# Routed attention and squared-ReLU layer, one core: the first head pair's loads, turns and one-hot rows rearranged

## The chip, the core and the metric

The kernel runs on one core of one Trainium2 chip. The metric is the device time of one execution in microseconds (us). Engines are named as the profile names them: PE is TensorE's matmul stream and PEld its weight loads, DVE is VectorE, ACT is ScalarE, POOL is GpSimd, and SP is SyncE, which here only issues DMAs. "SPq" and "ACTq" mark instructions that an engine's sequencer handles itself, above all DMA issues.

## What is computed

```python
q_n, k_n, c_n = each / (norm(each, axis=-1) + 1e-6)
q_assign = argmax(einsum('bhsd,hcd->bhsc', q_n, c_n), -1)   # nearest of 16 centroids
k_assign = argmax(einsum('bhsd,hcd->bhsc', k_n, c_n), -1)
scores = where(q_assign == k_assign, q @ k.T / sqrt(D), -1e9)
x = (softmax(scores) @ v)           # (4, 8, 768, 64) -> (3072, 512)
out = relu(x @ w_in) ** 2 @ w_out   # 512 -> 2048 -> 512
```

Batch 4, 8 heads, sequence 768, head width 64, all fp32.

## The kernel before

**Pairs.** The 32 (batch, head) problems are worked as 16 pairs of heads; the two heads of a pair share the 128 partitions. For each pair PE needs the queries and keys turned (head width on the partitions): the tile `qkT`, [128, 12, 128], 6 blocks of queries, then 6 of keys. From it come

- `logits(pair)` (L319): centroid scores of queries and keys; DVE turns them (`turn_logits`, L330) and finds the nearest centroid (`number`, L335);
- the mask, as a small matmul of rows that encode the centroid numbers (`mask`, L431). For pair 0 these rows are one-hot rows, turned on PE (`turn_onehot`, L378); for the others three rows per head that go through DRAM: `far` (L370) and then two DMAs into a `rows` tile (L373);
- `score` (L421), whose products PE adds in the same PSUM tile `sc`; then ACT's exponential (L442) and PE's product with v (`times_v`, L455), in the banks V and M.

There are three `sc` tiles of two PSUM banks each, and the two single banks V and M (`av_a`, `av_b` in the profile): eight banks together.

**Three ways to turn.** Pair 0 is turned on PE by `turn_first` (L259), pair 1 on PE by `turn` (L276), and from pair 2 on the DMA does it: `split_words` (L294) has ACT take the fp32 words apart into a tile `flat` and SP write it to DRAM (L303), once for the queries and once for the keys; `turn_words` (L310) reads both back with a transposing DMA (L314).

**The prologue.** SP and ACT issue the loads (L154 to L159): the centroids and the first keys on ACT's queue, everything else on SP's. POOL makes the identity `ident`, PE multiplies it by itself eight times (L170, the fp32 matmul is two records each, so 16 rows), and DVE fills constants, among them `oh` (L211) and two `rows` tiles (L218). Then, in the order in which they are written: `centroids_norm` (DVE, with a square root and a loaded exponential table on ACT), `turn_first(0)` for the queries, `turn_first(1)` for the keys, `centroids_turned` (one PE transpose into M, copied by DVE to `cnT`), `logits(0)`, `turn_logits(0)`, `number(0)`.

**What sets the order.** From L164 on, every engine's instructions stand in the order in which the program states them; semaphores are put in automatically. The loop of pairs is L575 to L660. For pair 0 the order is, after the loads of pair 3, three weight blocks and v of pair 1 on SP:

```python
for i in range(2):
    turn(1, i, (V, M)[i])
    score(p, i, 0, True)
split_words(2, 0)
turn_onehot()
turn(1, 2, V)
# masks and exponentials 0 to 2, logits(1), number(1), tiles 3 to 5
split_words(2, 1)
turn_words(2)
split_words(p + 3, 0)
# tiles 6 to 8
split_words(p + 3, 1)
load_qk(p + 4, (nc.scalar, nc.scalar))
round_1(p)
# times_v, evict, add_up; then pair 1: its tiles 0 to 2, logits(2), ...
```

`load_qk(4)` is issued by ACT; `round_1` (L128) is the first step of rounding a block of `w_in` on ACT; `evict` (L465) copies a finished product out of V or M. The tiles that take q, k and `flat` share six buffers (`loads`, tag `qk`).

After the 16 pairs come the two matrix products (L742 and L794), which are most of the time.

Of the kernel before, what the change touches and what calls it, by code (L numbers as in the profile page):

```python
# [8 lines left out]
F32 = mybir.dt.float32  # L9
BF16 = mybir.dt.bfloat16  # L10
# [3 lines left out]
ALU = mybir.AluOpType  # L14
# [4 lines left out]
P = 128  # L19
# [6 lines left out]
def kernel(  # L26
# [55 lines left out]
    def load_qk(pair, queues=(nc.sync, nc.sync)):  # L82
        if pair >= NG:
            return
        b, hp = divmod(pair, HP)
        raw[pair] = []
        for name, src, queue in zip(("q_raw", "k_raw"), (q, k), queues):
            t = loads.tile([P, 2, NCH, D], F32, name=name, tag="qk")
            queue.dma_start(
                t, src[b, 2 * hp : 2 * hp + 2].rearrange("h (p j) d -> p h j d", p=P)  # L90
            )
            raw[pair].append(t)
# [55 lines left out]
    def round_3(i):  # L148
        dst, lo, hi = of_block(i)
        raw_w.pop(i)  # L150
        dst, lo = dst.bitcast(I32), lo.bitcast(I32)
        nc.gpsimd.tensor_tensor(out=dst, in0=dst, in1=lo, op=ALU.add)  # L152

    cen = once.tile([P, D], F32, name="cen")  # L154
    nc.scalar.dma_start(cen, centroids.rearrange("h c d -> (h c) d"))
    load_qk(0, (nc.sync, nc.scalar))
    for pair in range(1, BY_PE + 1):
        load_qk(pair)
    load_v(0)  # L159

# [3 lines left out]
        tc.manual_schedule(engines={E.PE, E.DVE, E.Activation, E.Pool, E.SP})  # L164
    )

    ident = const.tile([P, P], F32, name="ident")
    make_identity(nc, ident)
    warm_up = ps_sc.tile([P, 2, 512], F32, name="sc")
    for _ in range(8):  # L170
        nc.tensor.matmul(warm_up[:, 0, 0:P], lhsT=ident, rhs=ident, start=True, stop=True)  # L171
    ident_b = const.tile([P, P], BF16, name="ident_b")
    nc.vector.tensor_copy(out=ident_b, in_=ident)
    ups = const.tile([P, D], F32, name="ups")
# [39 lines left out]
    marks = once.tile([P, 3, 32], BF16, name="marks")  # L214
    nc.vector.memset(marks, 0.0)
    rows_of = [once.tile([P, 2, S], BF16, name=f"rows_{i}") for i in range(2)]
    for t in rows_of:
        nc.vector.memset(t, 0.0)  # L218

    cnT = const.tile([P, H * C], F32, name="cnT")  # L220
    cn = const.tile([P, 2, D], F32, name="cen_n")
# [26 lines left out]
            )  # L248

    def centroids_turned():  # L250
        nc.tensor.transpose(
            out=M[:, 0:P], in_=cn.rearrange("p e d -> p (e d)"), identity=ident
        )
        nc.vector.tensor_copy(out=cnT, in_=M[:, 0:P])

    qkT = {}
    ohT = {}

    def turn_first(which):  # L259
        if which == 0:  # L260
            qkT[0] = qktp.tile([P, 2 * NCH, P], F32, name="qkT")
        pt = ps_sc.tile([P, 2, 512], F32, name="sc")
        for c in range(NCH):
            for e in range(2):
                nc.tensor.matmul(  # L265
                    pt[D * e : D * (e + 1), c // NB, (c % NB) * P : (c % NB + 1) * P],
                    lhsT=raw[0][which][:, e, c], rhs=ident, start=True, stop=True,
                )
        for i in range(2):
            copy = nc.vector.tensor_copy if which and i else nc.scalar.copy  # L270
            c = NCH * which + NB * i
            copy(out=qkT[0][:, c : c + NB].rearrange("p c n -> p (c n)"), in_=pt[:, i, 0:TB])
        if which == 1:
            raw.pop(0)

    def turn(pair, part, bank):  # L276
# [17 lines left out]
    def split_words(pair, which):  # L294
        if pair >= NG:
            return
        if which == 0:
            words[pair] = dram.tile([2 * NCH, P, 2, 2 * D], U16, name="words")
        flat = loads.tile([P, NCH, 2, 2 * D], U16, name="flat", tag="qk")
        src = raw[pair][which].bitcast(U16).rearrange("p h c (d two) -> p h c two d", two=2)  # L300
        for e in range(2):
            nc.scalar.copy(out=flat[:, :, :, D * e : D * (e + 1)], in_=src[:, e])
        nc.sync.dma_start(  # L303
            words[pair][NCH * which : NCH * (which + 1)].rearrange("c p two d -> p c two d"),
            flat,
        )
        if which == 1:
            raw.pop(pair)
# [10 lines left out]
    def logits(pair, bank):  # L319
        hp = pair % HP  # L320
        for g in range(4):
            nc.tensor.matmul(  # L322
                bank[32 * g : 32 * g + 32, 0, 0:TB], lhsT=cnT[:, 2 * C * hp : 2 * C * (hp + 1)],
                rhs=qkT[pair][:, NB * g : NB * (g + 1)], start=True, stop=True,
            )
# [52 lines left out]
    def turn_onehot():  # L378
        spare = expp.tile([P, 2, 512], F32, name="ex").bitcast(BF16)
        ohT[0] = spare.rearrange("p a n -> p (a n)")[:, 0 : 2 * S].rearrange(  # L380
            "p (a n) -> p a n", a=2
        )
        po = sc.pop("oh").rearrange("p a n -> p (a n)").bitcast(BF16)[:, 0 : NBL * P]
        po = po.rearrange("p (b g i) -> p b g i", b=NBL, g=4)
        for b in range(NBL):
            nc.tensor.transpose(
                out=po[:, b].rearrange("p g i -> p (g i)"),
                in_=oh[:, b].rearrange("p e c -> p (e c)"), identity=ident_b,
            )
        for which in range(2):  # L390
            dst = ohT[0][:, which].rearrange("p (g b i) -> p b g i", g=2, b=NBL)
            src = po[:, :, 2 * which : 2 * which + 2]
            if which == 0:
                nc.scalar.copy(out=dst, in_=src)
            else:
                nc.vector.tensor_scalar(
                    out=dst, in0=src, scalar1=BIG, scalar2=-BIG, op0=ALU.mult, op1=ALU.add
                )

# [14 lines left out]
    def begin(i):  # L416
        sc[i] = ps_sc.tile([P, 2, 512], F32, name="sc")
        return sc[i]
# [142 lines left out]
            loaded += 1  # L561

    centroids_norm()
    turn_first(0)
    turn_first(1)
    centroids_turned()
    logits(0, begin("ls"))
    for i in ("oh", 0, 1):
        begin(i)
# [5 lines left out]
    for p in range(NG):  # L575
        if p == 0:
            load_qk(3)
            load_ahead(0)
        if p == HP + 1:
            nc.sync.dma_start(x_far, xT.pop(0))  # L580
        if p:
            invert(p - 1)
            turn_words(p + 2)
            spread(p - 1)
        if 2 < p + 1 < NG:
            turn_logits(p + 1)
            number(p + 1)
        load_v(p + 1)
        if p:
            load_ahead(p - 1)  # L590


        if p == 0:
            for i in range(2):
                turn(1, i, (V, M)[i])
                score(p, i, 0, True)
            split_words(2, 0)
            turn_onehot()
            turn(1, 2, V)
            for i in range(NB):  # L600
                if i == 2:
                    begin(i)
                    score(p, i, 0, True)
                mask(p, i, 0, False)
                exponential(i)
        else:
            for i in range(NB):
                tile_of(p, i)
        total[p] = endp.tile([P, 2, S], F32, name="total")
        first, last = total[p][:, :, 0:QA], total[p][:, :, QA:S]  # L610
        add(nc.vector, first, ex[0], ex[1])
        if p < 2:
            logits(p + 1, begin("ls"))
            turn_logits(p + 1)
            number(p + 1)
        add(nc.vector, first, first, ex[2])
        for i in range(NB, NCH):
            tile_of(p, i)
            add(nc.vector, first, first, ex[i])
        if p == 0:  # L620
            split_words(2, 1)
            turn_words(2)
        split_words(p + 3, 0)


        for i in range(NCH, NCH + NB):
            tile_of(p, i)
        part = accp.tile([P, 2, 512], F32, name="part")
        add(nc.vector, part, ex[NCH], ex[NCH + 1])
        add(nc.vector, part, part, ex[NCH + 2])  # L630
        add(nc.vector, last, part[:, :, 0:QB], part[:, :, QB : 2 * QB])
        if p:
            finish(p - 1)
            round_2(p - 1)
            round_3(p - 1)
        split_words(p + 3, 1)
        load_qk(p + 4, (nc.scalar, nc.scalar))
        round_1(p)


        for i in range(NCH):
            times_v(p, i, V)
        evict(p, 0, V)
        for i in range(NCH, NCH + NB):
            times_v(p, i, M)
        raw_v.pop(p)
        if p + 1 < NG:
            bank = begin("ls")
            if 2 < p + 2:
                if p + 2 < NG:  # L650
                    logits(p + 2, bank)
            add_up(p, bank[:, 1])
        evict(p, NCH, M)
        for d in (qkT, ohT):
            d.pop(p)
        if p >= NG - 2:
            for _ in range(2):
                if (found := next(x_early)) is not None:
                    first_sums.append(found)
            w_early.append(w_sums(len(w_early)))  # L660
# [407 lines left out]
```

## Time and profile before

| | us |
|---|---|
| median of 3 runs (lowest to highest) | 913.22 (913.16 to 913.4) |
| the profiled execution: device time | 913.43 |
| its span, first to last instruction | 911.6 |
| PE busy | 899.4 |
| DVE, ACT, POOL busy | 581.7, 316.2, 150.1 |
| first matmul of `logits(0)` | 10.09 |
| first mask matmul of pair 0 | 17.49 |
| first matmul of `logits(2)` | 38.50 |

The difference between device time and span, 1.83 us, lies before the first and behind the last instruction. All times in the text are us from the first instruction. In rows of the timeline and the chain the first number is the start, the second the busy time. A row merges equal instructions; where the text goes into single instructions, it uses the trace's own rows. "Landed" is when a DMA's last semaphore increment stands in the trace.

### The profile page before, as it was taken

The numbers are of one execution on the slowest core, as the hardware profiler recorded it, in microseconds if no ns is written. First come the engines' busy times: TensorE is split into PE (matmuls) and PEld (weight loads), VectorE is DVE, ScalarE is ACT, GpSimd is POOL, SyncE is SP. The second block draws the span as 40 slices with busy tenths as digits, with TensorE's granted clock in tenths as the row PEclk, the third lists the DMA queues.
The fourth block names the chain that finished last, engine by engine and source line by source line (L and its number), as shares of the span: only waits on it lengthen the run. The fifth ranks groups of instructions, "written<-read, shape, count | busy, mean of one in ns | idle before, by whom it ended". The sixth has DMA issues, their size and how long they took to land.

```text
span 911.6 us, 11728 instructions
## 1 busy us (share of the span) xinstructions
PE 899.4 (99%) x4543; PEld 578.8 (63%) x4543; DVE 581.7 (64%) x930; ACT 316.2 (35%) x457; POOL 150.1 (16%) x168
## 2 busy tenths in 40 slices
PE   8999999999999999899999999999999999999997
PEld 5444444444444455478875568886558887557886
DVE  5798888888888999994326565225655333656321
ACT  5876677776776567530001110001110000111000
POOL 0000100001000267710023310023220003240000
PEclk9999999999999999999999999999999999999999
DMA  7677778777673154110000000000000000000000
GB/s 261 154 191 220 218 214 208 179 210 213 172 177 86 61 184 139 41 70 24 24 24 0 1 0 19 18 19 16 1 1 0 24 24 24 0 1 0 24 24 27
DMA packets 98482, 75.03 MB, mean 82 GB/s; under 512 B 54666, under 2 KB 89074, under 8 KB 98162
## 3 DMA queue, kind: packets, MB, share of 16 engines
q1 hardware_dynamic: 91474, 64.33, 24.9%
q10 hardware_dynamic: 6944, 9.86, 3.4%
q8 instruction: 38, 0.62, 0.3%
q14 instruction: 26, 0.21, 0.1%
HBM read 43.83 MB, written 19.34 MB: 69 GB/s over the span
## 4 chain that ended last, share of the span: by engine, by line
PE 92%; DVE 5%; issue 1%; ACT 1%; POOL 0%; DVEq 0%; POOLq 0%
PE bank L794 32%; PE bank L742 28%; PE sc L426 12%; PE av_a L459 9%; PE av_b L459 4%; PE sc L435 3%; PE sc L322 1%; DVE w_raw L137 1%; PE sc L478 1%; DVE g L699 1%; DVE w_raw L140 1%; DVE total L445 1%; DVE xT L510 0%; PE sc L171 0%; PE sc L265 0%
## 5 line engine op out<-in xcount | busy, mean ns | idle before, releaser
L699 DVE TENSOR_TENSOR g<-bank,g 128x384 f32<-128x384 f32 x192 | 102.9, 553 | 90.8 <-PE bank L742 88.6
L442 ACT ACTIVATE ex<-sc 128x1024 f32<-128x1024 f32 x144 | 144.2, 1025 | 39.0 <-PE sc L426 34.1
L426 PE MATMUL sc<-qkT 64*128 64x512 f32 (+1 forms) x768 | 150.6, 484 | 0.0
L794 PE MATMUL bank<-w_out,g 128*128 128x256 f32 x576 | 127.2, 379 | 0.0
L794 PEld LDWEIGHTS bank<-w_out,g 128*128 128x128 f32 x576 | 109.4, 190 | 15.7
L699 DVE TENSOR_TENSOR osb<-bank,osb 128x256 f32<-128x256 f32 x72 | 29.3, 422 | 136.5 <-PE bank L794 125.9
L742 PE MATMUL bank<-x_t,w_s 128*128 128x384 f32 x256 | 93.3, 487 | 3.1 <-POOL w_s L522 3.1
L742 PE MATMUL bank<-xT,w_in 128*128 128x384 f32 x256 | 93.2, 487 | 0.0
L742 PE MATMUL bank<-xT,w_s 128*128 128x384 f32 x256 | 93.0, 486 | 0.0
L426 PEld LDWEIGHTS sc<-qkT 64*128 64x128 f32 x768 | 65.9, 188 | 41.9 <-issue 30.1
L794 PE MATMUL bank<-w_t,g_s 128*128 128x256 f32 x384 | 86.8, 379 | 0.0
L794 PE MATMUL bank<-w_t,g 128*128 128x256 f32 x384 | 86.8, 379 | 0.0
L459 PE MATMUL av_a<-ex,v_raw 128*64 128x512 f32 x384 | 85.9, 596 | 0.0
L542 POOL TENSOR_TENSOR w_s<-w_in 128x256 f32<-128x256 f32 x32 | 26.7, 835 | 351.3 <-PE bank L794 235.4
L445 DVE TENSOR_TENSOR total<-total,ex 128x1024 f32<-128x1024 f32 x64 | 78.7, 1229 | 6.5
L705 ACT COPY osb<-bank 128x256 f32<-128x256 f32 x12 | 4.5, 372 | 216.1 <-PE bank L794 216.1
L794 PEld LDWEIGHTS bank<-w_t,g_s 128*128 128x128 f32 x384 | 73.0, 190 | 9.9
L794 PEld LDWEIGHTS bank<-w_t,g 128*128 128x128 f32 x384 | 73.0, 190 | 9.9
L705 ACT COPY g<-bank 128x384 f32<-128x384 f32 x32 | 15.3, 477 | 173.9 <-PE bank L742 173.9
L742 PEld LDWEIGHTS bank<-x_t,w_s 128*128 128x128 f32 x256 | 48.4, 190 | 37.9 <-POOL w_s L522 4.8
L152 POOL TENSOR_TENSOR w_in<-w_in,w_raw 128x512 int32<-128x512 int32 x16 | 22.1, 1378 | 296.4 <-DVE w_in L144 296.4
L742 PEld LDWEIGHTS bank<-xT,w_s 128*128 128x128 f32 x256 | 48.6, 190 | 33.9
(128 smaller groups left out, 1021.5 us busy)
## 6 DMA issues: line engine op xcount, KB each, us to landing
words<-flat SPq DMA_DIRECT2D x28, 384.0 KB
w_raw<-in_moe_w_in_dram SPq DMA_DIRECT2D x16, 512.0 KB
w_raw<-in_moe_w_out_dram SPq DMA_DIRECT2D x16, 512.0 KB
v_raw<-in_v_dram SPq DMA_DIRECT2D x16, 384.0 KB
rb<-far_r SPq DMA_DIRECT2D x32, 192.0 KB
out_dram<-osb SPq DMA_DIRECT2D x23, 256.0 KB
k_raw<-in_k_dram ACTq DMA_DIRECT2D x13, 384.0 KB
q_raw<-in_q_dram ACTq DMA_DIRECT2D x12, 384.0 KB
```

Of the source, the lines that this page charges most:

```text
L137: nc.vector.scalar_tensor_tensor(out=lo, in0=hi, scalar=0x80000000, in1=lo, op0=ALU.bitwise_and, op1=ALU.bitwise_or)
L152: nc.gpsimd.tensor_tensor(out=dst, in0=dst, in1=lo, op=ALU.add)
L426: nc.tensor.matmul(sc[i][:, e, cols], lhsT=qkT[pair][rows, NCH + c], rhs=qkT[pair][rows, n.start // P : n.stop // P], start=first, stop=no ...
L435: nc.tensor.matmul(sc[i][:, e, cols], lhsT=ohT[pair][rows, 1, c * P : (c + 1) * P], rhs=ohT[pair][rows, 0, columns(i)], start=first, stop= ...
L442: nc.scalar.activation(out=ex[i], in_=sc.pop(i), func=ACT.Exp, scale=SCALE)
L445: eng.tensor_tensor(out=out, in0=a, in1=b, op=ALU.add)
L459: nc.tensor.matmul(bank[D * e : D * (e + 1), 0 : n.stop - n.start], lhsT=raw_v[pair][:, e, c], rhs=ex[i][:, e, cols], start=c == 0, stop=c ...
L542: nc.gpsimd.tensor_tensor(out=s1, in0=a[1][0], in1=a[1][1], op=ALU.add)
L699: nc.vector.tensor_tensor(out=out, in0=bank, in1=to, op=ALU.add)
L705: nc.scalar.copy(out=c11, in_=bank)
L742: nc.tensor.matmul(bank, lhsT=operands[j][0][:, kk], rhs=operands[j][1][:, kk], start=(kk == 0), stop=(kk == H2 - 1),)
L794: nc.tensor.matmul(bank, lhsT=left[:, f], rhs=right[:, f], start=(f == 0), stop=(f == F2 - 1))
```

## The change

1. The first keys are loaded on SP's queue behind the first queries, and no longer on ACT's queue.
2. PE's eight first matmuls multiply a tile of zeros, filled by DVE's first instruction, and no longer wait for `ident`.
3. The two `rows` tiles (DVE, L218) are filled after `turn_onehot`, and no longer ahead of the centroids' norm.
4. `turn_first` works in halves of three blocks, each in a bank of its own: the queries in V and M, the keys in one bank each of two `sc` tiles. ACT copies the first three halves and DVE the last. The transpose of the centroids stands between the two halves of the keys, in the second bank of the tile of the first matmuls.
5. `turn_onehot` works in two halves of six blocks: the first in the `sc` tile's bank, copied by ACT (query rows and key rows), the second in M, copied by DVE (both).
6. `split_words(2, 0)` moves from ahead of `turn_onehot` to behind tiles 3 to 5, next to `split_words(2, 1)`; the two halves of pair 3 move behind tiles 6 to 8.

```diff
-    load_qk(0, (nc.sync, nc.scalar))
-    for pair in range(1, BY_PE + 1):
+    for pair in range(BY_PE + 1):
         load_qk(pair)
...
+    zeros = once.tile([P, P], F32, name="zeros")
+    nc.vector.memset(zeros, 0.0)
+    warm_up = ps_sc.tile([P, 2, 512], F32, name="sc")
+    for _ in range(8):
+        nc.tensor.matmul(warm_up[:, 0, 0:P], lhsT=zeros, rhs=zeros, start=True, stop=True)
     ident = const.tile([P, P], F32, name="ident")
     make_identity(nc, ident)
-    warm_up = ps_sc.tile([P, 2, 512], F32, name="sc")
-    for _ in range(8):
-        nc.tensor.matmul(warm_up[:, 0, 0:P], lhsT=ident, rhs=ident, start=True, stop=True)
...
-    for t in rows_of:
-        nc.vector.memset(t, 0.0)
...
+        turned = warm_up[:, 1, 0:P]
         nc.tensor.transpose(
-            out=M[:, 0:P], in_=cn.rearrange("p e d -> p (e d)"), identity=ident
-        )
-        nc.vector.tensor_copy(out=cnT, in_=M[:, 0:P])
+            out=turned, in_=cn.rearrange("p e d -> p (e d)"), identity=ident
+        )
+        nc.vector.tensor_copy(out=cnT, in_=turned)
...
+    def turn_first(which, i, bank, copy):
...
+        for c in range(NB):
             for e in range(2):
                 nc.tensor.matmul(
+                    bank[D * e : D * (e + 1), c * P : (c + 1) * P],
+                    lhsT=raw[0][which][:, e, NB * i + c], rhs=ident, start=True, stop=True,
                 )
+        c = NCH * which + NB * i
+        copy(out=qkT[0][:, c : c + NB].rearrange("p c n -> p (c n)"), in_=bank[:, 0:TB])
...
+        for half, bank in enumerate((sc.pop("oh")[:, 0], M)):
...
+                if half == 0:
+                    nc.scalar.activation(
+                        out=dst, in_=src, func=ACT.Copy,
+                        **({"scale": BIG, "bias": -BIG} if which else {}),
+                    )
+                elif which:
+                    nc.vector.tensor_scalar(
+                        out=dst, in0=src, scalar1=BIG, scalar2=-BIG, op0=ALU.mult, op1=ALU.add
+                    )
+                else:
+                    nc.vector.tensor_copy(out=dst, in_=src)
...
-    turn_first(0)
-    turn_first(1)
+    turn_first(0, 0, V, nc.scalar.copy)
+    turn_first(0, 1, M, nc.scalar.copy)
+    halves = [ps_sc.tile([P, 2, 512], F32, name="sc")[:, 0] for _ in range(2)]
+    turn_first(1, 0, halves[0], nc.scalar.copy)
     centroids_turned()
+    turn_first(1, 1, halves[1], nc.vector.tensor_copy)
...
-            split_words(2, 0)
             turn_onehot()
+            for t in rows_of:
+                nc.vector.memset(t, 0.0)
             turn(1, 2, V)
...
         if p == 0:
-            split_words(2, 1)
+            for i in range(2):
+                split_words(2, i)
             turn_words(2)
-        split_words(p + 3, 0)
+        else:
+            split_words(p + 3, 0)
...
+        if p == 0:
+            split_words(3, 0)
         split_words(p + 3, 1)
```

More of the change, by code (lines that the diff above doesn't have):

```diff
@@ L250, in centroids_turned @@
     def centroids_turned():
+        turned = warm_up[:, 1, 0:P]
         nc.tensor.transpose(
-            out=M[:, 0:P], in_=cn.rearrange("p e d -> p (e d)"), identity=ident
+            out=turned, in_=cn.rearrange("p e d -> p (e d)"), identity=ident
         )
-        nc.vector.tensor_copy(out=cnT, in_=M[:, 0:P])
+        nc.vector.tensor_copy(out=cnT, in_=turned)
     qkT = {}
     ohT = {}
-    def turn_first(which):
-        if which == 0:
+    def turn_first(which, i, bank, copy):
+        if which == 0 and i == 0:
             qkT[0] = qktp.tile([P, 2 * NCH, P], F32, name="qkT")
-        pt = ps_sc.tile([P, 2, 512], F32, name="sc")
-        for c in range(NCH):
+        for c in range(NB):
             for e in range(2):
                 nc.tensor.matmul(
-                    pt[D * e : D * (e + 1), c // NB, (c % NB) * P : (c % NB + 1) * P],
-                    lhsT=raw[0][which][:, e, c], rhs=ident, start=True, stop=True,
-                )
[L269 to L273, printed above, removed]
+                    bank[D * e : D * (e + 1), c * P : (c + 1) * P],
+                    lhsT=raw[0][which][:, e, NB * i + c], rhs=ident, start=True, stop=True,
+                )
+        c = NCH * which + NB * i
+        copy(out=qkT[0][:, c : c + NB].rearrange("p c n -> p (c n)"), in_=bank[:, 0:TB])
+        if which == 1 and i == 1:
             raw.pop(0)
@@ L382, in turn_onehot @@
         )
[L383 to L388, printed above, removed]
-            )
[L390 to L397, printed above, removed]
-                )
+        for half, bank in enumerate((sc.pop("oh")[:, 0], M)):
+            n = NBL // 2
+            blocks = slice(n * half, n * (half + 1))
+            po = bank.bitcast(BF16)[:, 0 : n * P].rearrange("p (b g i) -> p b g i", b=n, g=4)
+            for b in range(n):
+                nc.tensor.transpose(
+                    out=po[:, b].rearrange("p g i -> p (g i)"),
+                    in_=oh[:, n * half + b].rearrange("p e c -> p (e c)"), identity=ident_b,
+                )
+            for which in range(2):
+                dst = ohT[0][:, which].rearrange("p (g b i) -> p b g i", g=2, b=NBL)[:, blocks]
+                src = po[:, :, 2 * which : 2 * which + 2]
+                if half == 0:
[9 more added lines that the diff above has]
+                    nc.vector.tensor_copy(out=dst, in_=src)
     ex = {}
```

## The prediction, made before the changed kernel was run

> **What bounds the kernel.** I read the busy table first.
>
> ```profile
> PE 899.4 (99%) x4543; PEld 578.8 (63%) x4543; DVE 581.7 (64%) x930; ACT 316.2 (35%) x457; POOL 150.1 (16%) x168
> ```
>
> PE is busy nearly throughout, so an edit pays only where PE waits, or where it lets PE's unbroken stretch begin earlier. Then the chain of waits from 0 to 60 us:
>
> ```profile
> 1.36 3.78 PE sc L171 x16
> 5.14 3.51 PE sc L265 x48
> ...
> 8.68 0.49 ACT qkT L272
> 9.16 0.02 issue
> 9.19 0.56 DVE qkT L272
> 9.74 0.21 DVE cnT L254
> 9.95 0.14 issue
> 10.09 0.85 PE sc L322 x8
> ...
> 14.58 1.57 ACT flat L302 x2
> 16.14 0.71 ACT ex L394
> 16.85 0.02 issue
> 16.88 0.57 DVE ex L396
> 17.44 0.05 issue
> 17.49 0.61 PE sc L435 x4
> ```
>
> To 17.49 the chain changes hands between PE, ACT and DVE; from there it is PE alone for many pairs. Chain and PE's rows show later gaps only near 305 (0.26 us), 371 (1.7) and 382 (1.4), behind DVE's rounding, which itself started from a PE release at 284.86. So a shift of PE in the first pairs goes through to the end. In the steady pairs DVE idles 2.5 us of each 19.13, so DVE doesn't swallow it.
>
> One more place matters, read from the timeline of SP and of PE:
>
> ```profile
> 16.17 0.40 SPq L303 DMA_DIRECT2D words<-flat  x1
> 29.55 0.38 SPq L303 DMA_DIRECT2D words<-flat  x1
> 33.17 2.82 SPq L314 DMA_TRANSPOSE qkT<-words  x1
> 36.09 1.11 SPq L303 DMA_DIRECT2D words<-flat  x2
> 40.50 4.11 SPq L314 DMA_TRANSPOSE qkT<-words  x1
> ```
>
> ```profile
> 38.50 0.85 PE L322 MATMUL sc<-qkT,cnT 128*32 128x384 f32 x8
> ```
>
> The first four SP rows are pair 2's query words, its key words, its transposing DMA and pair 3's words. The PE row is logits(2), which reads what that transposing DMA writes. It landed at 38.10, PE's sequencer passed its semaphore at 38.18, and PE, still occupied by scores, began at 38.50: 0.3 us to spare, and no more.
>
> **The change part by part.**
>
> *First matmuls on zeros.* DVE fills 128 elements; between the memsets of 48 (0.098 us) and 768 (0.698) that is 0.165 us. The engines start at 0.74, and the fill's result reaches PE at about 0.95 instead of 1.36: 0.41 us earlier. The 16 rows then end 0.41 earlier, and the query turn's first weight load, at 5.07, could start at 4.66. The queries landed at 4.13, so they don't hold it up.
>
> How much of it lasts depends on the clock. PE's rows of the query turn come in pairs 0.213 us apart until 6.4 and 0.109 apart afterwards. If that step stays at 6.4, two more pairs run slow and 0.2 of the 0.41 remains; if it moves along with PE's first matmul, all 0.41. I carry 0.3.
>
> The Trainium skill, "TensorE: Matmul & The Clock Gate", section "What's actually happening", says that the fast state follows a busy window of about 3.4 us, and that the window runs free of the kernel. By that rule an earlier start could also make the window that ends near 3.0 count as busy; by an estimate from that page the first matmuls and the query turn would then be fast much sooner and logits(0) another 1.1 us earlier. The trace shows one step, 5 us after PE's first matmul, and can't say which window counts.
>
> *Key load, centroids, fills.* The first keys' issue (0.45 us) moves to SP and every later SP load issues 0.5 later; but the loads arrive 1.05 us apart, one after the other (6.39, 7.44, 8.50 ...), and their sum is the same. The first keys should land near 5.2 instead of 5.93, wanted at 6.8 or later. Nothing gained, nothing lost. The two `rows` fills (1.5 us) leave DVE ahead of the norm: the scaled centroids, ready at 7.87, are ready at 6.4, and ACT is free at 5.65 instead of 7.15. The chain above doesn't contain them, so alone that is worth nothing, but it covers the next edit. The fills go into DVE's idle time from 17.43 to 19.89, 2.46 us; without that cover they would cost 1.5.
>
> *Halves.* Before: the key turn ends at 8.62, DVE waits for ACT's copy until 9.19, copies (0.56), copies `cnT` (0.20 more), and logits(0) starts at 10.09. After: ACT has copied the third half before the last one is even turned, and `cnT` is copied meanwhile. Against it stands the centroids' transpose between the halves: L251 loads at 8.55 where the next turn would have come at 8.40, and ends at 8.88, so about 0.4 us is added ahead of the last half. With the 0.21 of a fixed clock step the last half ends at 8.78; +0.05 to DVE, +0.56 copy, +0.10 to PE: logits(0) at 9.49, 0.60 earlier. With the moved step 0.80. I carry **0.7**.
>
> *One-hot rows.* From logits(0) to the transposes at 15.04 PE runs without a stop, DVE's `oh` is ready 0.5 earlier, so everything there just shifts. From 15.04 on, unshifted: ACT no longer stands in the 1.57 us of splitting. First half's six transposes end at 15.55; ACT copies 384 elements twice (0.48 each by L272's row, 0.1 overlapped) to 16.44; DVE's two copies of the second half, about 0.36 each by L396's 0.56 for twice the elements, end at 16.56. Now PE is late: turn(1, 2) ends at 16.9, the mask starts at 16.83 instead of 17.49. Next ACT: its copy of turn(1, 2) runs to 17.54, so the first exponential starts at 17.44 instead of 17.92, and the mask of tile 3, which waits for the second exponential, at 19.42 instead of 19.91. **0.48** is gained, not the 0.66 of the mask.
>
> *Words later.* Both splits of pair 2 now stand behind exponential 5; there were two splits there before too ((2,1) and (3,0)), so exponentials 6 to 8 keep their place. Behind them two splits follow instead of one: ACT's round_1 and evicts come 1.57 us later, into its idle 1.38 and 1.59 us before pair 1's first exponential. Free.
>
> Not free is SP. Pair 2's query words were written at 16.17, long before. Now they queue behind `far` and `rows` of pair 1 and are issued at 29.55, the key words at 30.1. Two writes in a row took 4.3 us from the first issue to the last landing at 36.09 (40.41) and 4.2 at 52.36 (56.55); one took 3.6 at 29.55 (33.16), with ACT's q and k loads of pair 4 in flight. So the keys land near 33.75, 0.6 later than 33.16. The transposing DMA, issued on landing, took 4.93 us to land: 38.7 instead of 38.10. Against 0.3 us of slack PE then waits **0.3 us**, relative to everything else in its shifted place. Queued behind that wait on PE are logits(2), tiles 3 to 8 of pair 1 and all that follows; behind the transposing DMA on SP stand pair 3's words, the reciprocals and pair 2's `rows`, which had 1.4 us to spare (landed 53.80, wanted 55.26).
>
> ACT's loads of pair 4 come later as well, since their buffers are free later (issued 26.77 and 27.80 before; after pair 3's splits now, from about 31.5). One such load keeps the DMA engines about 1.05 us; the second falls on the transposing DMA. Bounds: 0 to 1.05, I take 0.5, the middle. So the stall is 0.8, with bounds 0 and, if the transposing DMA takes the 7.7 us of the one issued at 40.50, 3.1.
>
> **Sum.** 0.7 + 0.48 - 0.8 = 0.37 us. Profiled execution 913.43 - 0.37 = 913.06; the median of the runs lies 0.21 below it, so **912.85**.
>
> **The rivals.**
>
> *No stall.* The words land in time after all, for instance because ACT's delayed loads leave the DMA engines to them. For: the single write of before was slowed by just those loads. Against: two writes back to back took 4.2 and 4.3 us. 913.22 - 1.18 = 912.0.
>
> *A longer stall: slower than before.* One mechanism: pair 2's transposing DMA at logits(2). Its price passes the prologue's 1.18 us when it takes 5.9 us or more from issue to landing. For: of the first six, two took under 5.3 us, two 5.4 and 5.9, two 7.7 and 8.2, and it now meets ACT's loads. Against: in its place it took 4.93, and DVE and ACT are quiet there. With 6 to 7.7 us the time is 913.3 to 915.1; I name 914.0.
>
> *Clock earlier.* The other end for the query turn: wholly at the fast pace, from the landing at 4.13, 24 rows in 1.3 us; then the keys, whose second half waits for the centroids at 6.4. Logits(0) is then at 8.3, 1.8 earlier than before, and the sum 1.8 + 0.48 - 0.8 = 1.5: 911.7; without the stall 910.9. Against: in the trace the step came 5 us after PE's first row, and 0.41 of that is all that the change moves.
>
> *The halves don't part the engines.* DVE might wait for ACT as L272 and L396 do now ("DVE ex L396" waited 2.35 us for ACT). In the key turn ACT is done first anyway; in the one-hot rows DVE would end at 17.1, and the exponential gains 0.4 instead of 0.48. About 912.95.
>
> **Chances.** Forecast 0.47 (912.2 to 913.2), no stall 0.15, longer stall 0.25, clock earlier 0.08, engines not parted 0.05. The range reaches from the clock case to most of the long stall, 911.6 to 914.6, and leaves out 0.04 below and 0.12 above. A measurement of this kernel can tell about 0.2% (1.83 us) from no change. Faster than 911.39 needs the earlier clock and no or a small stall: 0.04. Slower than 915.05 is the long stall's end: 0.06. Within: 0.90.
>
> **What would show it.** PE's first row near 0.95; logits(0) near 9.4; the first exponential near 16.7; both words of pair 2 issued together near 28.4; then logits(2) not at the end of the scores but with an idle of some tenths ahead of it. It is wrong if that idle is absent, if logits(0) gains less than 0.4, or if DVE idles no more before the total at 19.9 and the fills hold it up.

## The result and the profile after

| kernel | median us (lowest to highest, runs) | ratio to before, 95% interval |
|---|---|---|
| before | 913.19 (912.85 to 914.0, 6) | |
| changed | 917.3 (916.84 to 917.93, 6) | 1.0043 [1.0032, 1.0054] |

The change costs about 4 us. The forecast was 912.85 with a range to 914.6: wrong in size and sign. The profiled execution of the changed kernel took 917.63 with a span of 915.9, against 913.43 and 911.6.

The edits moved lines: scores are now L432, the mask L441, the exponential L448, `times_v` L465, the words' write L301, the transposing DMA L312, `logits` L320, the exponential's sum `total` L451. First the chain of waits of the changed kernel (start, length, what):

```profile
8.08 1.49 PE sc L320 x8
...
16.17 1.85 ACT ex L448 x2
...
28.59 4.06 DMA words<-flat
...
32.70 7.07 DMA qkT<-words
...
39.91 1.51 PE sc L320 x8
41.41 0.54 PE sc L441 x2
41.95 1.71 PE sc L432 x4
...
50.24 5.30 PE av_a L465 x24
```

The prologue did gain: `logits(0)` ends at 9.57 (8.08 + 1.49) instead of 10.94, and the mask of tile 3 starts at 18.07 instead of 19.91, **1.84 us earlier**. In PE's timeline, before and after:

```profile
19.91 0.39 PE L435 MATMUL sc<-ex 64*128 64x512 bf16 x2
18.07 0.39 PE L441 MATMUL sc<-ex 64*128 64x512 bf16 x2
```

Part of the 1.84 is luck: PE's clock first rose at 4.93 in this execution and at 6.57 in the one before, which by the last section's 0.49 us per us is an estimated 0.8. But the chain then leaves PE for two DMAs and comes back at 39.91, at `logits(2)`; and what follows there is slow: 1.51 for the eight matmuls that took 0.85 before, 1.71 for four scores that take 0.86 elsewhere. The first product with v of pair 1 begins at 50.24 instead of 45.94. That is 4.30 late, and the span grew by 4.3: everything happens before 50 us, and all of it goes through to the end. The chain before, at the same two places:

```profile
38.57 0.78 PE sc L322 x8
...
45.94 5.30 PE av_a L459 x24
```

PE's timeline (the first row) and the windows (the other four) say how the 4.30 come about. The columns of the windows are length, then busy time of PE, PEld, DVE, ACT, POOL, then the granted clock, the DMA share and GB/s.

```profile
39.91 1.51 PE L320 MATMUL sc<-qkT,cnT 128*32 128x384 f32 x8 [3.18 <-DMA qkT<-words]
```

```profile
36.60:39.07 2.47, 0.13 (x2) 0.00 (x0) 1.23 (x1) 1.24 (x2) 0.00 (x0) 1.00 1.27 274
39.07:42.48 3.41, 2.57 (x12) 0.89 (x14) 0.97 (x2) 0.00 (x0) 0.00 (x0) 0.50 0.76 227
42.48:45.89 3.41, 3.41 (x12) 1.29 (x10) 3.20 (x10) 1.07 (x2) 0.00 (x0) 0.50 0.77 142
45.89:49.30 3.41, 3.41 (x34) 2.20 (x34) 3.20 (x3) 3.25 (x4) 0.00 (x0) 1.00 1.02 238
```

PE idles 3.18 us for the transposing DMA of pair 2. While it idles, its granted clock falls to 0.50 (1.00 is full speed) and stays there from 39.07 to 45.89; the work from `logits(2)` to the first product with v takes 10.33 us (39.91 to 50.24) where before it took 7.37 (38.57 to 45.94, by the chain). So, for this pair of executions: prologue **-1.84**, idle **+3.18**, halved clock **+2.96**, sum +4.30.

Why the DMA is late stands in the timelines of SP and ACT:

```profile
28.11 0.97 SPq L301 DMA_DIRECT2D words<-flat  x2
32.70 4.92 SPq L312 DMA_TRANSPOSE qkT<-words  x1
```

```profile
30.94 0.38 ACTq L89 DMA_DIRECT2D q_raw<-in_q_dram  x1
32.67 0.38 ACTq L89 DMA_DIRECT2D k_raw<-in_k_dram  x1
33.09 0.69 ACT L130 ACTIVATE w_in<-w_raw 128x512 f32<-128x512 f32 x1 [1.98 <-DMA words<-flat]
```

The two words writes of pair 2 were issued together, as foreseen, and landed at 30.92 and 32.65. ACT's load of pair 4's queries was issued at the first landing (30.94). At the second two DMAs set off at once: SP's transposing DMA (32.70), which reads the words, and ACT's load of pair 4's keys (32.67). The key load had waited on ACT for the same landing ("1.98 <-DMA words<-flat"), because its tile takes the buffer that the words are written from: q, k and `flat` share six buffers. The transposing DMA then took 7.07 us from issue to landing (39.77), against 4.93 before; the query load was still under way beside it until 34.36, the key load until 36.98. ACT's own wait is in no link of the chain.

### The profile page after: what moved, and what is told of

The parts are those of the page before. It is cut to its first block, busy times and chain, and to the rows that moved or that the text cites. A ratio compares the mean times of both kernels' runs of the same rounds, so it can differ in the third digit from the quotient of the medians.

```text
span 915.9 us, 11730 instructions
## 1 busy us (share of the span) xinstructions
PE 902.5 (99%) x4543; PEld 579.1 (63%) x4543; DVE 582.6 (64%) x932; ACT 316.0 (35%) x458; POOL 150.0 (16%) x168
## 4 chain that ended last, share of the span: by engine, by line
PE 90%; DVE 6%; DMA 1%; issue 1%; ACT 1%; POOL 0%; SPq 0%; DVEq 0%; ACTq 0%
PE bank L808 32%; PE bank L756 27%; PE sc L432 12%; PE av_a L465 8%; PE av_b L465 4%; PE sc L441 3%; PE sc L320 1%; DVE w_raw L137 1%; DVE g L713 1%; DVE w_raw L140 1%; PE sc L484 1%; DMA qkT<-words 1%; DVE total L451 1%; DVE xT L516 0%; DMA words<-flat 0%
## 5 line engine op out<-in xcount | busy, mean ns | idle before, releaser
L448 ACT ACTIVATE ex<-sc 128x1024 f32<-128x1024 f32 x144 | 144.0, 1025 | 43.0 <-PE sc L432 38.7
L432 PE MATMUL sc<-qkT 64*128 64x512 f32 (+1 forms) x768 | 152.3, 488 | 0.0
L432 PEld LDWEIGHTS sc<-qkT 64*128 64x128 f32 x768 | 66.6, 189 | 42.8 <-issue 30.8
L465 PE MATMUL av_a<-ex,v_raw 128*64 128x512 f32 x384 | 85.9, 596 | 0.0
L451 DVE TENSOR_TENSOR total<-total,ex 128x1024 f32<-128x1024 f32 x64 | 78.7, 1229 | 6.5
```

The costliest lines, as they stand in the source:

```text
L432: nc.tensor.matmul(sc[i][:, e, cols], lhsT=qkT[pair][rows, NCH + c], rhs=qkT[pair][rows, n.start // P : n.stop // P], start=first, stop=no ...
L448: nc.scalar.activation(out=ex[i], in_=sc.pop(i), func=ACT.Exp, scale=SCALE)
L451: eng.tensor_tensor(out=out, in0=a, in1=b, op=ALU.add)
L465: nc.tensor.matmul(bank[D * e : D * (e + 1), 0 : n.stop - n.start], lhsT=raw_v[pair][:, e, c], rhs=ex[i][:, e, cols], start=c == 0, stop=c ...
```

## The experiments

The theory after the result (A in the expectations): the sixth edit alone is the loss, by a long transposing DMA and by the clock that falls while PE waits; the five others gain. The rivals, as each expectation states them, put it elsewhere: on the other edits, on a transposing DMA that is slow by itself at that time, or on the idle time without the clock. All times were taken beside the kernel before (912.91 for the first four runs, 913.17 for the next four, 913.33 for the last two).

| kernel | median us | ratio to before, 95% interval |
|---|---|---|
| words back | 911.99 | 0.9987 [0.9978, 0.9996] |
| words only | 917.21 | 1.0038 [1.0024, 1.0052] |
| pair 4 loaded by SP | 912.87 | 0.9995 [0.9986, 1.0004] |
| PE kept busy, 7 | 918.07 | 1.0055 [1.0042, 1.0069] |
| PE kept busy, 3 | 914.5 | 1.0015 [1.0006, 1.0024] |
| words in the gap | 911.86 | 0.9985 [0.9976, 0.9994] |
| ident first | 912.22 | 0.9989 [0.9980, 0.9998] |
| fills first | 912.58 | 0.9994 [0.9985, 1.0003] |
| old one-hot rows | 912.4 | 0.9992 [0.9983, 1.0002] |
| old turns | 912.68 | 0.9990 [0.9981, 0.9999] |

### Words back: the sixth edit undone

```diff
+            split_words(2, 0)
             turn_onehot()
...
-            for i in range(2):
-                split_words(2, i)
+            split_words(2, 1)
             turn_words(2)
-        else:
-            split_words(p + 3, 0)
+        split_words(p + 3, 0)
...
-        if p == 0:
-            split_words(3, 0)
```

> The changed kernel with only its sixth edit undone: pair 2's query words are split and written ahead of turn_onehot again, pair 3's as before. Theory A (the loss is one chain: words written later, pair 2's transposing DMA late, PE idle at logits(2), then a halved clock; all other edits together gain the 1.84 us by which tile 3's mask came earlier): PE doesn't wait at logits(2), no clock step, 913.2 - 1.8 = 911.4 us, allowing 911 to 912.2. Rival B (something else in the rearranged prologue costs the time, the wait only shows it): it stays near 917.

911.99, within the 911 to 912.2 expected: faster than before, and 5.3 us below the changed kernel. The key words, alone on SP, took 3.0 us (28.11 to 31.13), the transposing DMA 4.99, and `logits(2)` follows the scores without a gap:

```profile
36.48 0.86 PE sc L432 x4
37.34 0.78 PE sc L320 x8
```

### Words only: the kernel before with the sixth edit alone

```diff
-            split_words(2, 0)
             turn_onehot()
...
-            split_words(2, 1)
+            for i in range(2):
+                split_words(2, i)
             turn_words(2)
-        split_words(p + 3, 0)
+        else:
+            split_words(p + 3, 0)
...
+        if p == 0:
+            split_words(3, 0)
         split_words(p + 3, 1)
```

> The kernel before with the sixth edit alone: both words of pair 2 behind tiles 3 to 5, pair 3's behind tiles 6 to 8. Theory A: the same wait of about 3.2 us at logits(2) and the same 3 us of halved clock, without the gain: 913.2 + 6.1 = 919.3 us, 917.5 to 920 by where the clock's step falls. Rival B: no loss from this edit, 913 to 914.

917.21, 4.3 us above the kernel before: this edit alone loses as much as the whole change (4.1), without any of the gains of the others. The chain repeats the changed kernel's links; the row behind it is of PE's timeline:

```profile
29.80 4.06 DMA words<-flat
33.88 0.03 issue
33.91 6.89 DMA qkT<-words
...
49.91 0.57 PE av_a L459
```

```profile
40.94 1.50 PE L322 MATMUL sc<-qkT,cnT 128*32 128x384 f32 x8 [2.46 <-DMA qkT<-words]
```

The idle time is 2.46 us and the clock is halved for one stretch of 3.41 us, not two. The first product with v comes 3.97 late (49.91 against 45.94): 2.46 of idle and 1.60 of slower work behind it (8.97 from `logits(2)` on, against 7.37), less the 0.09 by which PE came to the wait earlier. The time is below the 917.5 to 920 expected, which had added a wait of 3.2 us and two halved stretches.

### Pair 4 loaded by SP: no loads beside the transposing DMA

```diff
-        load_qk(p + 4, (nc.scalar, nc.scalar))
+        load_qk(p + 4, (nc.scalar, nc.scalar) if p else (nc.sync, nc.sync))
```

> The changed kernel with the loads of pair 4's queries and keys issued by SP, behind pair 2's transposing DMA and pair 3's words, instead of by ACT beside it. Theory A says that the transposing DMA took 7.07 us because one of those loads shared the DMA engines with it: now 4.9 to 5.3 us, PE idles about 1.0 us at logits(2) and the clock stays up: 913.2 - 1.84 + 1.0 = 912.4 us. Rival C (the transposing DMA is slow by itself when it is issued this late, or by ACT's and DVE's work beside it): 7 us again, 917.

On SP the two loads stand behind pair 3's words and are issued at 36.93 and 37.94. Everything else is as in the changed kernel, the pair of writes too:

```profile
28.66 4.06 DMA words<-flat
32.78 5.26 DMA qkT<-words
```

```profile
38.18 0.85 PE L320 MATMUL sc<-qkT,cnT 128*32 128x384 f32 x8 [1.00 <-DMA qkT<-words]
```

912.87, where 912.4 was expected and 917 by the rival. The transposing DMA took 5.26 instead of 7.07: **pair 4's loads beside it cost the transposing DMA some 1.8 us**. The run moves both loads, so it doesn't say what each of them costs. PE still idles 1.00 us, but the clock stays up (0.85 for the eight matmuls). The Trainium skill, "DMA: Bandwidth & Descriptors", section "Issuing engines are not separate DMA queues", says that DMAs of different issuers run on the same engines and interleave; 7.07 beside the loads and 5.26 without them agree with that.

### PE kept busy: the clock by itself

```diff
+        if p == 1:
+            for _ in range(7):
+                nc.tensor.matmul(V, lhsT=ident, rhs=qkT[1][:, 0:4], start=True, stop=True)
         if p < 2:
             logits(p + 1, begin("ls"))
```

> The changed kernel with seven matmuls of ident and queries of pair 1 into bank V ahead of logits(2), about 3.1 us of PE work whose result nobody reads: it fills PE's wait. Theory A, that the wait costs a second time through the clock: the wait stays 3.2 us, but the clock is not halved: 913.2 - 1.84 + 3.2 = 914.6 us. Rival D (the halved clock of the record costs nothing, or comes from elsewhere): 917.3 us as the changed kernel.

918.07, where 914.6 was expected: each of the 14 matmul records took 0.44 us, twice what I had sized them by; together they ran 6.21 us, longer than the wait they were to fill (PE came to it at 36.90, the transposing DMA landed at 39.31). The clock part showed all the same: it never fell, and `logits(2)` behind them took 0.78. Three of them fit:

> As the kernel with seven extra matmuls, but with three: there the 14 records took 6.2 us (0.44 each), twice what was wanted, so that PE was busy beyond the landing and the price of the clock couldn't be read. Three keep PE busy for 2.7 us, to about 39.6, where pair 2's transposing DMA lands near 39.3 to 39.8. Theory A (idle and clock are two separate losses): clock 1.0 throughout, the wait of about 3.2 us stays: 912.9 - 1.4 + 3.2 = 914.7 us, 914 to 915. Rival D (the clock isn't part of the loss): 917.3.

```profile
36.28 2.77 PE av_a L624 x6
39.05 0.11 issue
39.16 0.85 PE sc L320 x8
40.01 0.32 PE sc L441 x2
40.33 0.86 PE sc L432 x4
```

The wait is nearly the same (the transposing DMA ran from 32.15 to 39.02, 6.87 us; `logits(2)` begins 2.88 behind the scores), PE does useless work in it, and the four scores take 0.86 instead of 1.71. 914.5, within the 914 to 915 expected: **the halved clock is worth 2.8 us** of the changed kernel's 917.3, with some 1.3 us of doubt by the two intervals, and extra work on PE makes the kernel faster.

### Words in the gap

`split_words(2, 0)` and the loads of pair 3 are put behind `score(0, 0)`; the rest of the sixth edit is undone as above.

```diff
-            load_qk(3)
             load_ahead(0)
...
                 score(p, i, 0, True)
+                if i == 0:
+                    split_words(2, 0)
+                    load_qk(3)
```

> The changed kernel with pair 2's query words split and written between the copies of turn(1, 0) and turn(1, 1), where ACT idles 1.5 us, and the loads of pair 3 behind them (the buffers ask for it); the rest of the sixth edit undone. Theory A with the prediction's 0.48 us for the one-hot rows: both the early words and the free ACT ahead of the one-hot copies are had, so 0.5 us less than with the split ahead of turn_onehot (911.99): 911.5 us. Rival E (the split only moves the wait to turn(1, 1)'s copy): 912.0.

911.86, the fastest kernel measured, but its interval covers that of words back, and it can't part the 911.5 expected from the rival's 912.0. The trace can: the mask of tile 3 starts 8.50 us after the end of `logits(0)` in both (18.29 - 9.79, and 18.68 - 10.18), so the 0.5 us expected isn't there. With words back ACT's split stands in the chain ahead of the first mask:

```profile
13.82 1.57 ACT flat L300 x2
15.39 0.78 ACT ex L395 x2
16.21 0.60 PE sc L441 x4
```

Without it the first mask comes 0.13 sooner after `logits(0)` (15.47 - 9.57 in the changed kernel, against 16.21 - 10.18), and PE then waits for the second exponential: 8.50 there too. So beside the other edits the sixth had nothing to win.

### The first five edits, one at a time

These start from the kernel with the words back (911.99). All four intervals overlap its own, so the times alone part none of them from it; the traces say more. Ident first:

```diff
-    zeros = once.tile([P, P], F32, name="zeros")
-    nc.vector.memset(zeros, 0.0)
...
-        nc.tensor.matmul(warm_up[:, 0, 0:P], lhsT=zeros, rhs=zeros, start=True, stop=True)
     ident = const.tile([P, P], F32, name="ident")
     make_identity(nc, ident)
...
+        nc.tensor.matmul(warm_up[:, 0, 0:P], lhsT=ident, rhs=ident, start=True, stop=True)
```

> The kernel with the sixth edit undone (911.99), and with PE's eight first matmuls on ident again instead of zeros, so PE starts at 1.36 instead of 1.06. The prediction's reading: 0.2 to 0.4 us later, 912.2 to 912.4. Rival F (the step of PE's pace follows windows that don't move with the kernel, and its place in a run decides): within 0.15 us of 911.99, with the step anywhere.

912.22 (911.1 to 913.11 in 11 runs): +0.2, within the interval of nothing. Its profiled execution idles 0.40 us at `logits(2)`, where words back doesn't wait, so not even that is the first matmuls' alone. Fills first:

```diff
     rows_of = [once.tile([P, 2, S], BF16, name=f"rows_{i}") for i in range(2)]
+    for t in rows_of:
+        nc.vector.memset(t, 0.0)
...
             turn_onehot()
-            for t in rows_of:
-                nc.vector.memset(t, 0.0)
```

> The kernel with the sixth edit undone (911.99), and with the two rows tiles filled ahead of the centroids' norm again. The prediction's reading: the norm then ends at 7.9 instead of 6.4 and is late for the transpose between the key halves (L251, at 7.6 with the fills later): 0.3 us more, 912.3. Rival G (the fills cost nothing there either, or are worth their whole 1.5 us): 912.0 or 913.5.

912.58, about 0.6 more where 0.3 was expected, and in 11 runs it stays between 912.49 and 912.81. The chain shows DVE (with one link of 0.21 on ACT) leading to the keys' last half:

```profile
3.37 0.70 DVE rows L219
4.07 0.11 issue
4.18 0.70 DVE rows L219
...
7.33 0.55 DVE cen_n L246 x2
7.88 0.04 issue
7.92 0.33 PE sc L253
8.25 0.81 PE sc L267 x12
```

So the third edit is the cover of the fourth, as the prediction has it. Old one-hot rows (edit 5 undone) and old turns (edit 4 undone) put the code of before back in place of these functions:

```diff
-        for half, bank in enumerate((sc.pop("oh")[:, 0], M)):
...
+        po = sc.pop("oh").rearrange("p a n -> p (a n)").bitcast(BF16)[:, 0 : NBL * P]
+        for b in range(NBL):
...
+            if which == 0:
+                nc.scalar.copy(out=dst, in_=src)
```

> The kernel of the run in which pair 2's query words are split early again (911.99), and the one-hot rows are turned in one tile again, the query rows copied by ACT and the key rows by DVE. In that run's trace the time from the end of logits(0) to the mask of tile 3 was 8.50, as in the changed kernel, against 8.97 before. Theory A: the one-hot edit is worth these 0.47 by itself, with the split standing ahead of it on ACT: 912.46 (912.2 to 912.8), and the trace shows 8.9 to 9.0 from logits(0) to that mask. Rival F: the stretch became shorter for another reason (the rows fills, or logits(0)'s earlier place): 912.0 and 8.5.

912.4, +0.4; in the trace the mask of tile 3 starts 8.97 behind the end of `logits(0)` (18.94 - 9.97) instead of 8.50, as in the kernel before:

```profile
15.17 0.71 ACT ex L392
15.90 0.57 DVE ex L394
16.52 0.60 PE sc L433 x4
```

DVE waits for ACT again. These 0.47 are the 0.48 of the forecast.

```diff
-    turn_first(0, 0, V, nc.scalar.copy)
-    turn_first(0, 1, M, nc.scalar.copy)
-    halves = [ps_sc.tile([P, 2, 512], F32, name="sc")[:, 0] for _ in range(2)]
-    turn_first(1, 0, halves[0], nc.scalar.copy)
+    turn_first(0)
+    turn_first(1)
     centroids_turned()
-    turn_first(1, 1, halves[1], nc.vector.tensor_copy)
```

> The same kernel (911.99) with the turns of pair 0 and the centroids' transpose as they were before: whole tiles, the centroids behind both key halves. Theory A: the halves are worth about 0.5, because DVE waits for ACT's copy again and then copies the centroids: 912.5 (912.3 to 912.8), and logits(0) starts about 0.5 later than the other kernels do at the same place of the clock step (they start at 8.25 for a step at 5.28 and 8.69 for one at 6.18). Rival G: only the clock step decides when logits(0) starts, and the halves are worth nothing: 912.0.

912.68, +0.7 by the medians, but 0.3 by the ratios to the kernel before (0.9990 against 0.9987), and its profiled execution idles 0.20 at `logits(2)`. Its clock rose at 4.94, as in the changed kernel's profile (4.93), so the two compare: `logits(0)` ends at 9.98 instead of 9.57, the halves give 0.41.

## Why the prediction was wrong, point by point

- **The step that failed is the stall at `logits(2)`**, in its words "So the stall is 0.8". It was 3.18. The 2.4 that are missing come in three parts. *ACT's loads*: the prediction took 0.5, "the middle" of 0 to 1.05, as though a load delayed the transposing DMA by its own time at most. The transposing DMA took 7.07 where 4.93 + 0.5 was reckoned: 1.64 short. And the collision was no matter of chance: the load waits for the landing that also starts the transposing DMA. That could have been read from the six shared buffers. *The two writes*: 4.54 us from first issue to last landing, for the 4.2 taken from like pairs: 0.34. *SP's chain*: it was taken to move up as far as PE does. It came 1.44 earlier (29.55 to 28.11), PE 1.84, since `far` took 2.91 from issue to landing instead of 2.47: 0.40. This part is chance: in the changed kernel's order `far` took between 2.27 and 2.91 in the profiled executions. With the 0.8 these sum to 3.18. (The forecast's sum, 0.7 + 0.48 - 0.8, is 0.38 and not 0.37; nothing hangs on it.)
- **A term was absent**: PE's clock falls when PE idles long enough. The prediction's clock section looks only at the first rise. It is 2.96 us in the trace, 2.8 by the run with PE kept busy. Of the 5.3 us between the changed kernel and words back, 2.8 are the clock (917.3 to 914.5), about 1.6 the loads beside the transposing DMA (914.5 to 912.87), and about 0.9 the 1.00 us of idle that stays when only these loads are gone (912.87 to 911.99); that this idle comes from the writes that went out as a pair, and from `far`, is read from the trace and not tested alone. The intervals leave some 1.3 us of doubt on each difference, so the 0.9 is not clear of nothing.
- **The slower rival had the mechanism and the place**: "pair 2's transposing DMA at logits(2)", deciding from 5.9 us on. It took 7.07. Between its prices for 6 and 7.7 us that is 914.4 (the 913.3 for 6 us is 0.1 low by its own terms: 913.22 - 1.18 + 0.3 + 1.07), and the run without the clock's part measured 914.5. It deserved more than 0.25, and its price lacked the clock.
- **The sum passes through to the end**: right. 4.30 at 50 us, 4.3 in the span; with words back 1.23 earlier at tile 3 and at the first product with v of pair 1, 1.3 in the span.
- **One-hot rows, 0.48**: right in the trace (8.97 to 8.50 before tile 3, back to 8.97 when undone, with the split ahead of it on ACT each time); the time agrees (+0.4 when undone) but isn't clear of nothing. Without the split it is 0.35 (8.85 in words only, 8.50 in the changed kernel).
- **Halves**: right. With a fixed clock the terms give 0.39 to the halves (0.60 less the 0.21 of the first matmuls); 0.41 was measured in the trace at an equal clock; the time alone doesn't settle it.
- **First matmuls**: PE's first row came at 1.06, not 0.95, since DVE's first instruction started at 0.84. How much of the 0.30 lasts is not settled: +0.2 when undone, within the interval.
- **Key load, fills, splits on ACT**: free, as said. The first keys landed at 5.33 (5.2 foreseen). In the run with pair 4 loaded by SP the gain at tile 3 (1.40) less the longer gap at `logits(2)` gives the span's 0.3 within 0.1, so nothing else is lost.
- **Logits(0)**: 1.37 earlier in the profiled run against the 0.7 carried. The two alternatives of the forecast, a fixed or a moved clock step, were both wrong: the step lies elsewhere in each execution (last section). The rival "clock earlier" described this one execution, not the median: words back less the one-hot rows leaves about 0.5 (912.91 - 911.99 - 0.4).
- **No stall** would give 912.0, said that rival. Words back, which has no stall in its profiled execution, gives 911.99; but it takes undoing the sixth edit, and two kernels made from it idle 0.20 and 0.40 there.
- **The halves don't part the engines**, the last rival, is excluded by the trace: DVE's copies of the second half of the one-hot rows, at 14.63 and 14.90, wait for PE and not for ACT.

## What to carry to other kernels

When a transfer is moved next to its reader, list what else its landing sets free: a buffer that comes back at that moment starts the next load, and here that load and the reader's DMA set off within 0.03 us of each other. Price an idle stretch of PE at its length plus what the clock's fall may cost after it, and ask how much of one stretch of 3.41 us it takes up (next section). Taking one engine's work out of the chain (ACT's splits here) wins nothing when another wait ends as late, and its price lies in the queues that the moved work then stands behind.

## What the runs showed of the hardware

**The granted clock moves on a grid of 3.41 us, by the busy share of the stretch before.** In the changed kernel the clock's records are 34.133 us at full speed (ten times 3.4133), 6.827 at half (twice), then full. Shares of PE's busy time in the stretches of that grid, summed from the matmul rows of all twelve traces (before the first record, the slow pace of the matmuls stands for half):

| state | share of the stretch | clock of the next one |
|---|---|---|
| full | 0.47 to 0.65 (near 370, 380 and 905 us), 0.67, 0.68, 0.71 and more | full |
| full | 0.32 (changed), 0.33 (words only); 0.40 and less at the kernel's end | half |
| half | 0.54 and less, 0.75 | half |
| half | 0.84, 0.93, 0.95, 1.0 | full |

So the clock kept full speed after up to about 1.8 us of idle in one stretch (share 0.47) and lost it from about 2.05 us on (share 0.40); between them no run tells. At `logits(2)` an idle time of 1.00 us costs itself, one of 2.46 another 1.6, and one of 3.18 another 3.0, because the stretch in which PE came back was busy only to 0.75 and didn't raise the clock. The Trainium skill, "TensorE: Matmul & The Clock Gate", section "What's actually happening", has the window of 3413 ns and that it runs free of the kernel; the records agree. Its section "Why this matters for your kernels" asks for no idle gap above about 3 us; here a gap of 2.46 us, 2.29 of them within one stretch, was enough to lose the clock.

**Where that grid lies differs from run to run.** The first rise stood between 3.91 and 6.64 in the profiled executions, and `logits(0)` starts about 0.49 later for each us of it in the changed kernel's order (8.08 at 4.93, 8.69 at 6.18). The other kernels' times scatter by 0.9 to 2.3 us; the one with the fills first, where DVE and not PE leads to the last half of the keys, scatters by 0.32, which fits.

**A transposing DMA beside a load.** The same transfer, pair 2's, took 4.84 to 5.26 us in the eight profiled executions in which none of pair 4's loads was in flight during its first 4 us, and 6.87 to 7.07 in the four with pair 4's key load issued within 0.03 us of it and its query load in flight for the first 1.6 to 1.7. Why these loads cost it 1.6 to 2.2 us, more than the 1.05 by which prologue loads follow each other, no run here shows.
